# Identity and mask built by the vector engine, and new durations in the table that orders the instructions (linear attention and two gated MLPs, one core)

## The chip, the core and the metric

The kernel runs on one NeuronCore of a Trainium2 chip. A core has five engines that run side by side, each with its own instruction queue in order: TensorE (PE, matrix products, its weight loads are shown as PEld), VectorE (DVE), ScalarE (ACT), GpSimd (POOL) and SyncE (SP, which here issues all DMAs). They wait for each other through semaphores. The metric is the device time of one execution in microseconds (us).

## The reference

Three stages follow each other. Attention with a decaying state, per batch and head (4 batches, 8 heads, 768 steps, head dimension 48):

```
for t in range(S):
    state = alpha[:, :, t, :, None] * state + einsum('bhd,bhe->bhde', k[:, :, t], v[:, :, t])
    y[:, :, t] = einsum('bhd,bhde->bhe', q[:, :, t], state)
```

Then 3072 tokens of width 384 go through `x / rms * rms_g`, and `(silu(xn @ w_gate) * (xn @ w_val)) @ w_out` with an inner width of 1536, and then through `max(x @ w1, x @ w2, x @ w3) @ w_out` with an inner width of 768. All data is float32; the weights lie in memory as 64-bit numbers.

## The kernel before

**Attention** is done in 24 tiles of 128 time steps (6 for each of 4 batches, batches alternating). For a tile, the decays, keys and queries are loaded (`in_al`, `in_kk`, `in_qq`). For tiles 0 to 5 PE turns them (L570, transposes against `ident`); from tile 6 on DVE turns them (L576). DVE then runs a backward product scan (L598, writes `R`) and scales the keys (L604); this step is called `br`. The step `b` is a reciprocal, a forward scan (L611) and the scaling of the queries (L621). PE turns the keys back (L637) and forms the scores (L644); DVE masks them with `mask` (L657, `at`); PE multiplies with the values (L667, L676, L682), which gives the tile's output and the state's update (DVE L701 or L705). ACT sums the squares of the output, POOL makes the inverse root from it (L693, L696), DVE normalises (L710, `xn`), PE turns the tile (L716), and ACT and DVE split it into a high and a low half, `xh` (L723) and `xl` (L727).

**The first MLP** works on blocks of 384 tokens, which are three tiles. It goes through 96 slots; in a slot PE forms the gate product (nine matrix products, three splits over three parts of the width, L760 with `wg`), the value product (L760 with `wv`) and, later, the second product (L807). Between them ACT applies silu (L790), DVE multiplies (L793, tile `sg`), and ACT (L797) and DVE (L801, tile `hl`) split the result. The first two blocks alternate: slots 0 to 5 are block 0 with the first six of twelve column groups, slots 6 to 11 block 1 with the same six, slots 12 to 23 both with the other six. **The second MLP** has 48 slots of three products and a second product (L960).

**Weights** come in as chunks of 64-bit words (`raw`, L360). DVE rebuilds a float from each word (three instructions a chunk, L58 to L60, done for two chunks at once and called a join), ACT rounds it to the high half (L374), DVE makes the low half (L380), and ACT checks ranges (L389, L392).

**What sets the order.** Nothing in the kernel issues in the order of the loops. Every step is entered in a table with `plan.add(name, engine, cost, due, needs, run, ...)`; `Order.run` plays the table through with these costs: whenever an engine is free it takes the step with the lowest due time among those whose needs are met. The order in which steps start in this play is the order in which each engine's instructions are issued. On the chip each engine then follows its list strictly. Where PE would be free before the value product of slot 0, the play inserts a filler product (L767, a product of `ident` and `mask` whose result is not used) and reckons 0.11 us for it.

**The constants.** `ident` and `mask` (the upper triangle with the diagonal) are made on POOL by two library helpers: a memset each, and a select along a diagonal (masks.py:199 and masks.py:66). In POOL's list a row `ISA` stands ahead of the first select; it is the only one of its kind between the kernel's start and the last reduction.

Of the kernel before, what the change touches and what calls it, by code (L numbers as in the profile page):

```python
# [10 lines left out]

F32 = mybir.dt.float32
F32R = mybir.dt.float32r
# [5 lines left out]
ALU = mybir.AluOpType  # L19
# [4 lines left out]
B, H, S, D = 4, 8, 768, 48  # L24
DM, F1, F2 = 384, 1536, 768
P = 128
# [255 lines left out]
def gla_moe_moe(ctx: ExitStack, tc: tile.TileContext, q, k, v, alpha, wg, wv, wo, g, w1, w2, w3, wo2, out):  # L282
    nc = tc.nc
# [29 lines left out]
    plan = Order()  # L313
# [8 lines left out]
    class Weights:  # L322


        def __init__(self, tag, pool, bufs, chunks, where, due, needs):

            self.tag, self.pool, self.raws, self.tmps = tag, pool, {}, {}
            self.chunks, self.where = chunks, where
            n = len(chunks)
            first = tag == "w1"  # L330
            for i in range(n):
                at = due(i) - 10 - (HEAD[i // 2] if first and i < 8 else 1.5)
                before = needs(i) + self.prev("load", i, 1) + self.prev("check", i, bufs)
                if i >= bufs:
                    before.append((tag, "join", (i - bufs) // 2 * 2))
                plan.add((tag, "load", i), "SP", 1.1, at, before, partial(self.load, i, bufs), later=LAT)
            for i in range(0, n, 2):
                both = [j for j in (i, i + 1) if j < n]
                at = due(i) - (HEAD[i // 2] if first and i < 8 else 1 if first else 1.5)
                plan.add((tag, "join", i), "DVE", 1.3 * len(both), at,  # L340
                         [(tag, "load", j) for j in both] + self.prev("rest", i, 2) + self.prev("join", i, 2),
                         partial(self.join, both))
                plan.add((tag, "high", i), "ACT", 0.42 * len(both), at, [(tag, "join", i)] + self.needed(needs, both),
                         partial(self.high, both))
                plan.add((tag, "rest", i), "DVE", 0.47 * len(both), at + 0.2, [(tag, "high", i)],
                         partial(self.low, both))
                for j in both:
                    plan.add((tag, "check", j), "ACT", 1.14, at + 2, [(tag, "load", j)],
                             partial(self.check, j))

        def prev(self, kind, i, n):
# [72 lines left out]
    pa = ExitStack()  # L424
    ap1 = pa.enter_context(tc.tile_pool(name="ap1", bufs=1, side="right", reuse_waits="tile"))
    ap = pa.enter_context(tc.tile_pool(name="ap", bufs=2, side="right", reuse_waits="tile"))

    ident = ap1.tile([P, P], F32, name="ident")
    mask = ap1.tile([P, P], F32, name="mask")
    half = ap1.tile([P, 1], F32, name="half")  # L430
    gb = ap1.tile([P, DM], F32, name="gb")
    ins, halves = [], []
    for nm, fill in (("al", 1.0), ("kk", 0.0), ("qq", 0.0)):
        t = ap1.tile([P, 2 * H * 64], F32, name=f"in_{nm}")
# [10 lines left out]
    for t in (R, ends):  # L445
        nc.gpsimd.memset(t[:, :, P - 1:P], 1.0)
    St = [ap1.tile([W, NP, D], F32, name=f"S{b}") for b in range(B)]
    make_identity(nc, ident)
    make_upper_triangular(nc, mask, val=1.0, diag=True)
    nc.gpsimd.memset(half, -0.5)  # L450
    xh, xl = {}, {}
    order = list(range(8))
# [12 lines left out]
    def room(n):  # L465
        def count(_, started):
            return 3 if ("g", 0) in started else 6 if n >= TPB else 7
        return count
# [7 lines left out]
    class Tile_:  # L476


        def __init__(self, n):
            self.n, self.s, self.c0 = n, n % 2, n * NSTAT  # L480
            self.b, self.c = tiles[n]
            self.blk, self.j = divmod(n, TPB)
            c, last = self.c, self.c == NC - 1

            if n < TPB:
                at, step = -20 + 2 * n, 0.5
            elif n < 2 * TPB:
                at, step = -10 + 0.5 * (n - TPB), 1
            elif n < 3 * TPB:
                at, step = 12 + 3 * (n - 2 * TPB), 1  # L490
            else:
                at, step = 21 + 4 * (n - 3 * TPB), 0.7

            def t(kind, m=n):
                return ("t", kind, m) if m >= 0 else None

            def add(kind, engine, cost, i, needs, run, **kw):
                last_one = t(kind, n - 1)
                needs = needs + [last_one if last_one in plan.parts else None]
                plan.add(t(kind), engine, cost, at + step * i, needs, run, **kw)  # L500

            r = room(n)
            self.pe = n < NPE
            if n <= NPE:
                old = [t("pa", n - 2), t("pa", n - 1) if n == NPE else None]
            else:
                old = [t("bt", n - 1)]
            add("ld", "SP", 3.3, -2, old, self.load, later=LAT)
            add("lv", "SP", 1.1, -1, [t("pc", n - 2), t("ld")], self.load_v, later=LAT)
            if self.pe:  # L510
                plan.add(t("pa"), "PE", 1.31, at + 0.5, [t("ld"), t("pa", n - 1), t("pc", n - 2)], self.pe_a, banks=3,
                         until=[t("b")], room=r)
            free = [t("b", n - 1), t("pb", n - 2), t("pc", n - 2), t("sqb", n - 2)]
            if not self.pe:
                add("bt", "DVE", 1.85, 0.9, [t("ld")] + free, self.pre_bt)
            add("br", "DVE", 1.6, 1, [t("pa" if self.pe else "bt")] + free, self.pre_br)
            add("b", "DVE", 2.1 if c else 1.8, 1, [t("br")] + ([t("st", n - B)] if c else []) +
                ([t("st", n - 2)] if n < NT - B + 2 else []), self.pre_bq)
            add("sqb", "ACT", 1.48, 1.5, [t("b")], self.post_b)
            add("pb", "PE", 1.75 if last else 2.13, 1.5, [t("b"), t("pc", n - 1)], self.pe_b,  # L520
                banks=2 if last else 3, until=[t("c")] + ([] if last else [t("kn")]), room=r)
            if not last:
                add("kn", "ACT", 0.45, 2, [t("pb"), t("pc", n - 1)], self.copy_kn)
            add("c", "DVE", 1.25, 2, [t("pb"), t("pc", n - 1)], self.pre_c)
            add("pc", "PE", (1.4 if c else 0.9) + (0 if last else 0.5), 2.5,
                [t("c"), t("lv"), None if last else t("kn")], self.pe_c, banks=1 if last else 2,
                until=[t("d")] + ([] if last else [t("st")]), room=r)
            add("ss", "ACT", 0.42, 3, [t("pc")], self.norm)
            add("rr", "POOL", 0.6, 3, [t("ss")], self.root)
            if not last:  # L530
                add("st", "DVE", 0.54, 3, [t("pc")], self.pre_st)
            add("d", "DVE", 0.5, 3.1, [t("rr"), t("pc"), t("pd", n - 3), "gb"], self.pre_d)
            free = [("v", last_of[self.blk - 2])] if self.blk > 1 else []
            add("pd", "PE", 0.33, 3.5, [t("d")] + free, self.pe_d, banks=1, until=[t("el")], room=r)
            add("eh", "ACT", 0.42, 4, [t("pd")], self.split_h)
            add("el", "DVE", 0.47, 4, [t("eh")], self.split_l)
# [358 lines left out]
    n = len(chunks1)  # L895
# [10 lines left out]
    for blk in range(NBLK):  # L906
# [5 lines left out]
        at = NS + (blk - 1) * NF2 + 1 if blk else NS - 6  # L912
        final = max(pi for pi, p_ in enumerate(passes) if p_[0] == blk)
        if blk > 1:
            free = ("p", (blk - 1) * NF2 - 1, 2)
        else:
            free = ("v", last_of[NBLK - 2 + blk])
        plan.add(("yf", blk), "SP", 1.64, at, [("yst", final, i) for i in range(KT)] + [free] +
                 ([("yf", blk - 1)] if blk else []), fetch, later=2.2)
        for i in range(KT):  # L920
# [8 lines left out]
            n = blk * KT + i  # L929
# [120 lines left out]
```

## Time and profile before

| | us |
|---|---|
| median of 3 runs | 926.93 |
| lowest and highest of them | 926.07, 927.68 |
| the profiled execution's own time | 927.05 |
| its span (first to last instruction) | 925.2 |
| PE busy | 888.6 (96%) |
| DVE busy | 527.4 (57%) |
| ACT busy | 353.4 (38%) |
| POOL busy | 24.3 (3%) |

The span is 1.85 us shorter than the execution's time. The busy shares are means over stages with different limits: in the first 100 us DVE is busy almost without a gap, later PE is. In the chain of work that ended last, PE holds 84% and DVE 7%.

### The profile page before, as it was taken

To read this page: it belongs to the slowest core of one execution; us is meant where nothing else is said; L and a number is where in the kernel's file an instruction comes from. 1 tells how busy PE (TensorE), PEld (TensorE's weight loads), DVE (VectorE), ACT (ScalarE), POOL (GpSimd) and SP (SyncE) were. 2 spreads that over 40 slices of the span, in tenths; PEclk is the share of its full clock that TensorE was granted. 3 is DMA by queue.
4 is the path that set the end of the run, shared out by engine and by line. 5 is a ranking of instruction groups with operands and counts; after the bars stand their busy time and mean duration, and the time that the engine had idled before them with its cause. 6 is when DMAs were issued, how large, how long until landed. Compare 5 with 4: busy or idle time off the path is not lost.

```text
span 925.2 us, 16299 instructions
## 1 busy us (share of the span) xinstructions
PE 888.6 (96%) x6477; PEld 864.7 (93%) x6477; DVE 527.4 (57%) x1052; ACT 353.4 (38%) x898; POOL 24.3 (3%) x70
## 2 busy tenths in 40 slices
PE   4899699899999999999999999999999999999997
PEld 3789699799999999999999999999999999999997
DVE  3999978987666666666666258465333323323222
ACT  3568577432333333333223258553222212212121
POOL 1001000000000000000000000000000000000000
PEclk9999799999999999999999999999999999999999
DMA  8745454533223223222221025221100101101000
GB/s 170 130 125 172 129 187 120 146 108 82 56 57 82 57 56 83 56 57 82 57 56 53 1 86 182 92 99 39 52 26 27 52 1 52 39 13 52 1 26 28
DMA packets 106241, 69.14 MB, mean 75 GB/s; under 512 B 49200, under 2 KB 103856, under 8 KB 106160
## 3 DMA queue, kind: packets, MB, share of 16 engines
q1 hardware_dynamic: 106160, 68.05, 26.8%
q8 instruction: 52, 0.85, 0.4%
q14 instruction: 29, 0.24, 0.1%
HBM read 57.41 MB, written 10.62 MB: 74 GB/s over the span
## 4 chain that ended last, share of the span: by engine, by line
PE 84%; DVE 7%; DMA 2%; ACT 1%; issue 1%; POOL 0%; SPq 0%; DVEq 0%; POOLq 0%; ACTq 0%
PE bank L760 53%; PE bank L807 14%; PE bank L960 8%; PE bank L644 2%; PE bank L682 2%; PE bank L676 2%; DMA raw<-in_moe_w_dram 1%; DMA raw<-in_moe_w_val_dram 1%; PE bank L667 1%; DVE cv_t L59 1%; PE bank L716 1%; DVE aT L611 1%; DVE cv_t L60 1%; PE bank L637 1%; DVE sg L793 1%
## 5 line engine op out<-in xcount | busy, mean ns | idle before, releaser
L945 DVE TENSOR_TENSOR sg<-sg,bank 128x384 f32<-128x384 f32 x96 | 53.2, 554 | 171.6 <-PE bank L760 168.3
L793 DVE TENSOR_TENSOR sg<-sg,bank 128x384 f32<-128x384 f32 x96 | 52.8, 551 | 104.2 <-PE bank L760 103.5
L797 ACT ACTIVATE hh<-sg 128x384 fp32r<-128x384 f32 x96 | 50.2, 523 | 150.6 <-DVE sg L793 150.5
L760 PE MATMUL bank<-xh,wvh 128*128 128x384 f32 x288 | 98.7, 343 | 7.3 <-DVE sg L793 4.3
L760 PE MATMUL bank<-xh,wgh 128*128 128x384 f32 x288 | 100.8, 350 | 0.0
L760 PE MATMUL bank<-xh,wvl 128*128 128x384 f32 x288 | 97.7, 339 | 1.6 <-DVE wvl L380 1.6
L760 PE MATMUL bank<-xh,wgl 128*128 128x384 f32 x288 | 97.2, 337 | 1.5 <-DVE wgl L380 1.5
L807 PE MATMUL bank<-hh,woh 128*128 128x384 f32 x288 | 98.5, 342 | 0.0
L807 PE MATMUL bank<-hl,woh 128*128 128x384 f32 x288 | 96.7, 336 | 1.8 <-DVE hl L801 1.8
L760 PE MATMUL bank<-xl,wvh 128*128 128x384 f32 x288 | 97.4, 338 | 0.0
L760 PE MATMUL bank<-xl,wgh 128*128 128x384 f32 x288 | 97.1, 337 | 0.0
L807 PE MATMUL bank<-hh,wol 128*128 128x384 f32 x288 | 96.4, 335 | 0.0
L949 ACT ACTIVATE hh<-sg 128x384 fp32r<-128x384 f32 x48 | 25.2, 525 | 160.2 <-DVE sg L945 160.2
L801 DVE TENSOR_TENSOR hl<-sg,hh 128x384 fp32r<-128x384 f32 x96 | 53.3, 555 | 32.1 <-ACT hh L797 32.1
L790 ACT ACTIVATE sg<-bank 128x384 f32<-128x384 f32 x96 | 46.6, 486 | 47.2 <-PE bank L760 46.7
L760 PEld LDWEIGHTS bank<-xh,wvh 128*128 128x128 f32 x288 | 54.8, 190 | 9.8 <-DVE sg L793 6.4
L760 PEld LDWEIGHTS bank<-xh,wvl 128*128 128x128 f32 x288 | 54.9, 191 | 2.2 <-DVE wvl L380 2.2
L807 PEld LDWEIGHTS bank<-hl,woh 128*128 128x128 f32 x288 | 54.1, 188 | 2.7 <-DVE hl L801 2.7
L760 PEld LDWEIGHTS bank<-xh,wgl 128*128 128x128 f32 x288 | 54.6, 190 | 1.8 <-DVE wgl L380 1.8
L807 PEld LDWEIGHTS bank<-hh,woh 128*128 128x128 f32 x288 | 54.2, 188 | 2.0
L760 PEld LDWEIGHTS bank<-xh,wgh 128*128 128x128 f32 x288 | 54.8, 190 | 1.3
L760 PEld LDWEIGHTS bank<-xl,wvh 128*128 128x128 f32 x288 | 54.9, 191 | 0.0
(137 smaller groups left out, 2004.3 us busy)
## 6 DMA issues: line engine op xcount, KB each, us to landing
raw<-in_moe_w_out_dram SPq DMA_DIRECT2D x18, 384.0 KB, 3.9
raw<-in_moe_w_dram SPq DMA_DIRECT2D x18, 384.0 KB, 3.9
y_scr<-yo SPq DMA_DIRECT2D x30, 192.0 KB, 2.0
raw<-in_moe_w_gate_dram SPq DMA_DIRECT2D x12, 384.0 KB, 4.0
vt<-in_v_dram SPq DMA_DIRECT2D x24, 192.0 KB, 2.6
raw<-in_moe_w_val_dram SPq DMA_DIRECT2D x12, 384.0 KB, 3.8
xl<-y_scr SPq DMA_DIRECT2D x8, 576.0 KB, 4.3
out_dram<-yo SPq DMA_DIRECT2D x24, 192.0 KB, 1.9
```

The costliest lines, as they stand in the source:

```text
L644: nc.tensor.matmul(self.sc[i][:, pr, :], self.kT[lo:hi, pr, :], self.qT[lo:hi, pr, :], start=True, stop=True)
L676: nc.tensor.matmul(self.y[tk, 2 * pr:2 * pr + 2, :].rearrange("p a d -> p (a d)"), self.qT[:, pr, tk], Sds[self.s][:, pr, :], start=True, ...
L682: nc.tensor.matmul(self.y[tk, 2 * pr + i, :], at[i][:, pr, tk], vt[:, 2 * pr + i, :], start=not self.c, stop=True, skip_group_check=True,)
L760: nc.tensor.matmul(ps, w_[:, kt, col], m_[:, kt, :], start=i == 0, stop=i == 3 * KT - 1)
L790: nc.scalar.activation(hid[s], banks[3][:, :NB], AF.Silu)
L793: nc.vector.tensor_tensor(hid[s], hid[s], banks[4][:, :NB], ALU.mult)
L797: nc.scalar.activation(hi_[s], hid[s], AF.Copy)
L801: nc.vector.tensor_tensor(lo_[s], hid.pop(s), hi_[s].bitcast(F32), ALU.subtract)
L807: nc.tensor.matmul(banks[e][:, :NB], w_[:, f, es], m_, start=f == f0 and i == 0, stop=f == f1 - 1 and i == 2)
L945: nc.vector.tensor_tensor(hid2[z], hid2[z], banks[3 + j][:, :NB], ALU.max)
L949: nc.scalar.activation(hi2[z], hid2[z], AF.Copy)
L960: nc.tensor.matmul(banks[t][:, :DM], l_[:, tsl], r_[:, f, :], start=f == 0 and i == 0, stop=f == NF2 - 1 and i == 2)
```

## The change

`ident` and `mask` are built on DVE instead of POOL. A row of ones is scanned into a running count `column` (0, 1, 2, ... along the free dimension), a 32-wide transpose of it gives each partition its own number within a group of 32 (`place`), and for each group of 32 partitions one comparison writes the group's rows of `ident` (equal) and one those of `mask` (greater or equal). That is one memset, one scan, one transpose and eight comparisons on DVE; the two helpers' instructions leave POOL.

The second part changes costs in the table: eleven numbers, no need, due time or buffer.

```diff
-    make_identity(nc, ident)
-    make_upper_triangular(nc, mask, val=1.0, diag=True)
+    column = ap1.tile([P, P], F32, name="column")
+    place = ap1.tile([P, 32], F32, name="place")
+    nc.vector.memset(mask, 1.0)
+    nc.vector.tensor_tensor_scan(column, mask, mask, -1.0, ALU.mult, ALU.add)
+    nc.vector.transpose(place, column[:, 0:32])
+    for t, op in ((ident, ALU.is_equal), (mask, ALU.is_ge)):
+        for lo in range(0, P, 32):
+            nc.vector.tensor_scalar(
+                t[lo:lo + 32], column[lo:lo + 32], float(lo), place[lo:lo + 32, 0:1], ALU.subtract, op
+            )
...
-            add("br", "DVE", 1.6, 1, [t("pa" if self.pe else "bt")] + free, self.pre_br)
+            add("br", "DVE", 2.3, 1, [t("pa" if self.pe else "bt")] + free, self.pre_br)
...
-            add("sqb", "ACT", 1.48, 1.5, [t("b")], self.post_b)
+            add("sqb", "ACT", 1.95, 1.5, [t("b")], self.post_b)
```

The other costs: a chunk's high half 0.42 to 0.45, its check 1.14 to 1.42, `b` 2.1 to 2.7 (1.8 to 2.15 for a batch's first tile), `c` 1.25 to 1.2, `ss` 0.42 to 0.65, `rr` 0.6 to 0.85, `st` 0.54 to 0.75, `d` 0.5 to 0.54.

What this does to the lists, at three places. First POOL's list at the start (`half` is a constant of one column, `r` the inverse root of a tile). Before, and then after:

```order
L446 MEMSET ends 112x4
masks.py:197 MEMSET ident 128x128
masks.py:199 ISA
masks.py:199 AFFINE_SELECT ident<-ident 128x128
masks.py:65 MEMSET mask 128x128
masks.py:66 AFFINE_SELECT mask<-mask 128x128
L450 MEMSET half 128x1
L693 TENSOR_SCALAR r<-stats 128x1
```

```order
L446 MEMSET ends 112x4
L459 MEMSET half 128x1
L702 ISA
L702 TENSOR_SCALAR r<-stats 128x1
L705 TENSOR_TENSOR r<-r,half 128x1
```

The `ISA` row stands now ahead of the first inverse root. It waits for no semaphore; the instruction behind it waits for ACT.

Second, DVE's list ahead of the first gate product, which needs the third tile's `xl`. Before, with tile 4's steps `br` and `b` whole ahead of `xl`, and after (line numbers are 9 higher):

```order
L598 SCALAR_TENSOR_TENSOR R<-bank_74,ends 112x511
L603 TENSOR_SCALAR least<-R 112x4
L604 TENSOR_TENSOR kT<-bank_75,R 112x512
L608 RECIPROCAL starts<-least 112x4
L610 TENSOR_TENSOR all<-all,least 112x4
L611 SCALAR_TENSOR_TENSOR aT<-bank_74,starts 112x512
L617 TENSOR_TENSOR Sd_117<-S_125,all 48x4x48 x2
L621 TENSOR_TENSOR qT<-bank_78,aT 112x512
L727 TENSOR_TENSOR xl<-bank_76,xh 128x3x128
```

```order
L607 SCALAR_TENSOR_TENSOR R<-bank_74,ends 112x511
L612 TENSOR_SCALAR least<-R 112x4
L613 TENSOR_TENSOR kT<-bank_75,R 112x512
L736 TENSOR_TENSOR xl<-bank_79,xh 128x3x128
L617 RECIPROCAL starts<-least 112x4
L619 TENSOR_TENSOR all<-all,least 112x4
L620 SCALAR_TENSOR_TENSOR aT<-bank_74,starts 112x512
L626 TENSOR_TENSOR Sd_117<-S_125,all 48x4x48 x2
L630 TENSOR_TENSOR qT<-bank_78,aT 112x512
```

Tile 4's step `b` has moved behind that `xl`. On PE the fillers ahead of the first gate product are 191 instead of 141.

Third, DVE's list around the multiplication of slot 5 (the row with `sg`), which PE's value product of slot 6 waits for. Before and after:

```order
L380 TENSOR_TENSOR wvl<-cv_t,wvh 128x3x128
L380 TENSOR_TENSOR wol<-cv_t,woh 128x384
L58 TENSOR_SCALAR cv_t<-raw 128x384 x2
L59 SCALAR_TENSOR_TENSOR cv_t<-raw,cv_t 128x384 x2
L60 SCALAR_TENSOR_TENSOR cv_t<-raw,cv_t 128x384 x2
L608 RECIPROCAL starts<-least 112x4
L610 TENSOR_TENSOR all<-all,least 112x4
L611 SCALAR_TENSOR_TENSOR aT<-aT,starts 112x512
L617 TENSOR_TENSOR Sd_117<-S_127,all 48x4x48 x2
L621 TENSOR_TENSOR qT<-qT,aT 112x512
L793 TENSOR_TENSOR sg<-sg,bank_77 128x384
L380 TENSOR_TENSOR wgl<-cv_t,wgh 128x3x128
```

```order
L380 TENSOR_TENSOR wvl<-cv_t,wvh 128x3x128
L380 TENSOR_TENSOR wol<-cv_t,woh 128x384
L58 TENSOR_SCALAR cv_t<-raw 128x384 x2
L59 SCALAR_TENSOR_TENSOR cv_t<-raw,cv_t 128x384 x2
L60 SCALAR_TENSOR_TENSOR cv_t<-raw,cv_t 128x384 x2
L736 TENSOR_TENSOR xl<-bank_80,xh 128x3x128
L802 TENSOR_TENSOR sg<-sg,bank_77 128x384
L585 STREAM_TRANSPOSE aT<-in_al 128x4x4x32
L585 STREAM_TRANSPOSE kT<-in_kk 128x4x4x32
L585 STREAM_TRANSPOSE qT<-in_qq 128x4x4x32
L380 TENSOR_TENSOR wgl<-cv_t,wgh 128x3x128
L380 TENSOR_TENSOR wvl<-cv_t,wvh 128x3x128
```

All of tile 6 (three transposes, `br` and `b`) stood ahead of the multiplication of slot 5 before; now all of it stands behind.

On PE, what lies between the score products of tile 4 (L644) and the gate product of slot 3 was, before, the second and value products and then tile 4's value products and a turn (L667 to L716); after the change the gate product of slot 3 follows the scores of tile 4 at once.

## Rows read from the trace of the kernel before

**Rows 1.** The page: busy time, share of the span, instructions of PE
```profile
PE 888.6 (96%) x6477; PEld 864.7 (93%) x6477; DVE 527.4 (57%) x1052; ACT 353.4 (38%) x898; POOL 24.3 (3%) x70
```
**Rows 2.** PE's waits, 0 to 60 us: us in all, times, longest
```profile
PE bank L570 <- POOL ident masks.py:199: 13.7, 1, 13.7
```
**Rows 3.** Timeline of POOL: start, duration, instruction, idle before and its releaser
```profile
13.31 0.28 POOL masks.py:199 TENSOR_SCALAR_AFFINE_SELECT ident<-ident 128x128 f32<-128x128 f32 x1 [9.64 <-issue]
...
26.19 0.19 POOL L693 TENSOR_SCALAR r<-stats 128x1 f32<-128x1 f32 x1 [12.02 <-ACT junk L471]
```
**Rows 4.** Timeline of SP's DMA issues at the start
```profile
0.74 0.45 SPq L542 DMA_DIRECT2D in_al<-in_alpha_dram  x1
...
11.41 0.43 SPq L561 DMA_DIRECT2D vt<-in_v_dram  x1
14.78 0.37 SPq L542 DMA_DIRECT2D in_al<-in_alpha_dram  x1
```
**Rows 5.** DMA issues, 0 to 2.5 us: count, KB each, us to landing
```profile
in_al<-in_alpha_dram SPq DMA_DIRECT2D x1, 192.0 KB, 3.3
```
**Rows 6.** Timeline of DVE up to the first gate product
```profile
14.79 0.16 DVE L595 COPY all<-bank 112x4 f32<-112x4 f32 x1 [14.79 <-PE bank L570]
...
15.20 1.22 DVE L598 TENSOR_TENSOR_SCAN R<-bank,ends 112x511 f32<-112x511 f32 x1
...
19.27 0.62 DVE L58 TENSOR_SCALAR cv_t<-raw 128x384 int32<-128x384 int32 x2
...
20.74 1.02 DVE L60 SCALAR_TENSOR_TENSOR cv_t<-raw,cv_t 128x384 int32<-128x384 int32 x2
...
53.25 0.17 DVE L608 RECIPROCAL starts<-least 112x4 f32<-112x4 f32 x1
...
55.93 0.55 DVE L727 TENSOR_TENSOR xl<-bank,xh 128x384 fp32r<-128x384 f32 x1
```
**Rows 7.** Busy time of L767 alone: stretch, length, PE, PEld, clock, DMA, GB/s
```profile
0.00:56.70 56.70, 18.52 (x141) 14.41 (x141) 0.97 0.72 147
```
**Rows 8.** Busy time of all engines: PE, PEld, DVE, ACT, POOL, then clock
```profile
0.00:60.00 60.00, 42.25 (x492) 37.09 (x492) 42.89 (x92) 28.90 (x83) 6.74 (x27) 0.97 0.68 139
```
**Rows 9.** Timeline of PE: the first gate product
```profile
56.72 0.42 PE L760 MATMUL bank<-xh,wgh 128*128 128x384 f32 x1
```
**Rows 10.** PE's waits, 56 to 200 us
```profile
PE bank L760 <- DVE sg L793: 3.4, 2, 3.0
PE bank L760 <- ACT wvh L374: 2.8, 1, 2.8
PE bank L760 <- DVE wvl L380: 1.6, 1, 1.6
PE bank L760 <- DVE wgl L380: 1.5, 1, 1.5
PE bank L807 <- DVE hl L801: 1.5, 2, 1.3
```
**Rows 11.** The chain that ended last: start, duration, what
```profile
109.06 6.12 PE bank L760 x18
...
116.75 3.12 PE bank L760 x18
```
**Rows 12.** Busy time of all engines, columns as in rows 8
```profile
100.00:105.00 5.00, 3.54 (x11) 3.54 (x12) 3.49 (x10) 1.87 (x6) 0.00 (x0) 0.52 0.95 258
...
200.00:300.00 100.00, 100.00 (x838) 96.88 (x838) 68.39 (x132) 33.10 (x85) 2.95 (x8) 1.00 0.30 78
```
**Rows 13.** Timeline of DVE around the multiplication of slot 5
```profile
93.43 1.09 DVE L576 STREAM_TRANSPOSE aT<-in_al 128x512 f32<-128x512 f32 x1
...
105.77 0.17 DVE L608 RECIPROCAL starts<-least 112x4 f32<-112x4 f32 x1
...
108.46 0.55 DVE L793 TENSOR_TENSOR sg<-sg,bank 128x384 f32<-128x384 f32 x1
```
**Rows 14.** PE's waits, 200 us to the end
```profile
PE bank L807 <- DVE hl L801: 0.4, 1, 0.4
```

More of the change, by code (lines that the diff above doesn't have):

```diff
@@ L9 @@
 from concourse.bass import ds
-from concourse.masks import make_identity, make_upper_triangular
+from concourse.masks import make_identity
 F32 = mybir.dt.float32
@@ L342, in __init__ @@
                          partial(self.join, both))
-                plan.add((tag, "high", i), "ACT", 0.42 * len(both), at, [(tag, "join", i)] + self.needed(needs, both),
+                plan.add((tag, "high", i), "ACT", 0.45 * len(both), at, [(tag, "join", i)] + self.needed(needs, both),
                          partial(self.high, both))
@@ L347, in __init__ @@
                 for j in both:
-                    plan.add((tag, "check", j), "ACT", 1.14, at + 2, [(tag, "load", j)],
+                    plan.add((tag, "check", j), "ACT", 1.42, at + 2, [(tag, "load", j)],
                              partial(self.check, j))
@@ L515, in __init__ @@
                 add("bt", "DVE", 1.85, 0.9, [t("ld")] + free, self.pre_bt)
-            add("br", "DVE", 1.6, 1, [t("pa" if self.pe else "bt")] + free, self.pre_br)
-            add("b", "DVE", 2.1 if c else 1.8, 1, [t("br")] + ([t("st", n - B)] if c else []) +
+            add("br", "DVE", 2.3, 1, [t("pa" if self.pe else "bt")] + free, self.pre_br)
+            add("b", "DVE", 2.7 if c else 2.15, 1, [t("br")] + ([t("st", n - B)] if c else []) +
                 ([t("st", n - 2)] if n < NT - B + 2 else []), self.pre_bq)
-            add("sqb", "ACT", 1.48, 1.5, [t("b")], self.post_b)
+            add("sqb", "ACT", 1.95, 1.5, [t("b")], self.post_b)
             add("pb", "PE", 1.75 if last else 2.13, 1.5, [t("b"), t("pc", n - 1)], self.pe_b,
@@ L523, in __init__ @@
                 add("kn", "ACT", 0.45, 2, [t("pb"), t("pc", n - 1)], self.copy_kn)
-            add("c", "DVE", 1.25, 2, [t("pb"), t("pc", n - 1)], self.pre_c)
+            add("c", "DVE", 1.2, 2, [t("pb"), t("pc", n - 1)], self.pre_c)
             add("pc", "PE", (1.4 if c else 0.9) + (0 if last else 0.5), 2.5,
@@ L527, in __init__ @@
                 until=[t("d")] + ([] if last else [t("st")]), room=r)
-            add("ss", "ACT", 0.42, 3, [t("pc")], self.norm)
-            add("rr", "POOL", 0.6, 3, [t("ss")], self.root)
+            add("ss", "ACT", 0.65, 3, [t("pc")], self.norm)
+            add("rr", "POOL", 0.85, 3, [t("ss")], self.root)
             if not last:
-                add("st", "DVE", 0.54, 3, [t("pc")], self.pre_st)
-            add("d", "DVE", 0.5, 3.1, [t("rr"), t("pc"), t("pd", n - 3), "gb"], self.pre_d)
+                add("st", "DVE", 0.75, 3, [t("pc")], self.pre_st)
+            add("d", "DVE", 0.54, 3.1, [t("rr"), t("pc"), t("pd", n - 3), "gb"], self.pre_d)
             free = [("v", last_of[self.blk - 2])] if self.blk > 1 else []
```

## The prediction

> **What bounds the kernel now.** I read the page's busy times first. PE holds 96% of the span [rows 1], so what can be won is PE's idle time, its fillers, and stretches at a low clock; the useful products stay as they are. Then PE's waits. The longest by far is the first: 13.7 us until `ident` is there [rows 2]. POOL's timeline tells why: ahead of the select that writes `ident` POOL is idle for 9.64 us and waits for nothing that the profile shows [rows 3]; the only thing between its memset and the select is the `ISA` row of its list. The inputs come much earlier: the first tile's `in_al` is issued at 0.74 and lands 3.3 later, at 4.04 [rows 4, 5].
>
> From there DVE runs the first tiles. It starts at 14.79 [rows 6] and the first gate product, slot 0, at 56.72 [rows 9]; from 0 to 60 us DVE is busy for 42.89 of the 45.2 us that it has left then [rows 6, 8]. So the head is DVE's, with PE filled up by 141 fillers [rows 7]. After slot 0 PE waits 3.4 + 2.8 + 1.6 + 1.5 + 1.5 = 10.8 us up to 200 us, all of it for steps that DVE makes or feeds [rows 10], and pays for these waits a second time in clock: a piece of 18 products takes 6.12 us right after such a wait and 3.12 later [rows 11], 3.0 us more, which is the lower of the two clock levels (1.2 instead of 2.4 GHz); from 100 to 105 us the granted clock is 0.52 for 3.54 us of PE work [rows 12], some 1.7 us more. Together 15.5 us lost after slot 0. Behind 200 us PE is full, with DVE at 68% [rows 12] and one wait of 0.4 us of note [rows 14]; nothing is to be won there.
>
> **Part 1, the constants.** DVE's eleven instructions stand at the head of its list, where it is idle until 14.79. None is in the trace, so bounds from its own rows: a scan of 511 columns takes 1.22 and a transpose of 512 columns 1.09, a comparison-like operation on 384 columns 0.31 (two in 0.62) [rows 6, 13]. Taken whole, memset, scan, transpose and four comparisons for `ident` are at most 1.22 + 1.22 + 1.09 + 4 x 0.31 = 4.8 us; scaled by columns (128, 128, 32, 128) they are about 0.3 + 0.3 + 0.1 + 0.4 = 1.1. I take 2, near the scaled end, since the operands are a quarter as wide. With a start at about 0.7 `ident` is there near 3 (at most 5.5). PE then waits for the inputs, 4.04, and starts 9.6 us earlier than at 13.7 [rows 2]. The cover of the new work is thus the first load; if the upper bound holds it costs 1.5 us. `mask` follows within another us and is needed only after the first scores.
>
> What is late next? Two sums, of which the larger sets slot 0.
> DVE: it starts 14.79 - 13.7 = 1.1 after PE, at 5.2. Before, from 14.79 to the end of the third `xl` (55.93 and 0.5) it took 41.6 us [rows 6]. Tile 4's step `b`, 53.25 to 55.93, now stands behind that `xl`: 41.6 - 2.7 = 38.9, so 44.1, and a little more for the second weight chunk, whose landing now comes after DVE is ready for it.
> PE: from 13.7 to 56.72 it was busy for 42.25 less the 3.3 us past slot 0's start, 39.0, of which 18.52 were fillers: 20.5 us of work [rows 7 to 9]. There are 50 fillers more, at 18.52 / 141 = 0.13 or less each, 5 to 6.5 us: 20.5 + 18.5 + 6 = 45 from 4.04, so 49. Part of the old 39.0 ran at the low clock (the mean of 0.97 over 60 us is 1.8 us of it) and would shrink with more fillers: 47.2. I take 47.5 for slot 0, PE's own sum with its fillers as the bound: 9.2 us earlier. Both ends stay for the range: 45 and 49.
>
> **Part 2, the order.** The clearest row is the multiplication of slot 5, at 108.46, for which PE waited 3.0 us and after which it ran at half clock [rows 10, 11, 13]. Ahead of it in DVE's list stood all of tile 6: three transposes from 93.43 on (about 0.95 each, 2.8), and `br` and `b`, 4.5 us as for tile 0 from 14.79 to 19.27 [rows 6, 13]; the first row of `b` is at 105.77. These 7.3 us now stand behind it. Of the waits of [rows 10] the 3.0, 2.8 and 1.6 all lie in this stretch (95 to 109 us) and all come from this order: DVE did tile 6 while the weights for slot 5 waited. They go, with the clock that they cost.
>
> In their place others come, since DVE's total is the same. The one that I can work out is the gate product of slot 3. From the multiplication of slot 1 DVE has ahead of that slot's low halves one join (19.27 to 21.76, 2.5), tile 5's `br` and `b` (4.5, and 0.7 for the carried state), a multiplication, a low half and two low halves of weights (0.5 each): 9.7 us [rows 6]. PE has meanwhile what is left of slot 2's gate product (1.4), a second and a value product (1.56 each, half of 3.12 [rows 11]) and tile 4's scores (1.6): 6.1. It then waits 3.5 us where before it had tile 4's value products to do. Following the lists on in the same way I find four more waits of 0.6 to 1.7 us up to slot 17, 4.5 us in sum, an estimate. So 15.5 - 8.0 = 7.5 us won, if the clock holds through the 3.5 us; if it falls, 3.0 less. At least nothing is won, at most 15.5.
>
> **Sum.** Against the profiled execution's own 927.05 us (its span is 925.2; the median of the runs is 926.93, 0.1 less): 9.2 for the head and 7.5 for the order give 910.4; against the median 910.3. I forecast 910.3.
>
> **A rule weighed.** The `ISA` row now stands right ahead of the first inverse root and has no wait of its own. By the trace it began as soon as POOL's memsets were done and took 9.64 us [rows 3]; beginning at about 3.5 it is over at 13, and the first inverse root, at 26.19 before, is due at about 19 then: hidden. The Trainium skill (GPSIMD Engine Reference, 2.1 Instruction dispatch) says that the first call of a freshly loaded kernel pays about 6 us for loading its code. If that is paid at the call, it falls on the first inverse root's path, which is the fourth rival below. The trace before cannot tell the two apart, since there the call stood right behind the `ISA` row.
>
> **Rivals.**
> 1. The order wins nothing: as much new waiting as old. Then only the head is left, 927.05 - 9.2 = 917.9. For it: DVE's sum up to 100 us is unchanged, and a busy DVE makes one wait of another. Against: 7.3 us of work really leave the way of slot 5.
> 2. The new costs fit so well that no wait after slot 0 is left: 927.05 - 9.2 - 15.5 = 902.4. Against: slot 3's 3.5 us.
> 3. The start is the loads'. The third tile's loads, issued at 14.78, were held by PE's first transposes; now they follow the issue at 11.41 on SP [rows 4], 2.9 us earlier and no more. If everything hangs on them, 924.1. Against: that tile's transposes ran long after its loads had landed.
> 4. The POOL code is loaded at its first call. The first `xn` on DVE, which stands in order ahead of tile 2, comes 9.64 - 0.5 = 9.1 us late and takes the head's gain: 927.05 - 9.2 + 9.1 - 7.5 = 919.4, and 3.0 more for the clock of an idle PE, 922.4.
> 5. Slower: the order of the later stage is worse. Behind 200 us PE waits for next to nothing, and the new costs move `xl` ahead of a `hl` there (0.5 us a tile). If each of the 16 last attention tiles made PE wait for `hl` by as much as the longest such wait before, 1.3 us [rows 10], it would lose 20.8: 931.1. It decides from (16.7 + 1.9) / 16 = 1.2 us a tile on. Against: DVE's 32% of idle time there [rows 12] and a single wait of 0.4 [rows 14].
>
> **How the numbers follow.** Chances: the forecast (906 to 914) 0.47, rival 1 (to 921) 0.24, rival 2 (below 906) 0.14, rival 3 0.05, rival 4 0.05, rival 5 0.05. A measurement of this kernel tells 0.2%, 1.9 us, from no change. Faster by more: all of the forecast, of rivals 1, 2 and 4, and most of 3: 0.93; within 0.2%: 0.03; slower: 0.04. The range for 8 in 10 goes from 901.5 (slot 0 at 45 or so and few waits) to 922 (rival 1 with slot 0 at 49 and a lost clock). The likeliest case alone is 906 to 914.
>
> **What would show it.** In the profile after: no wait of PE for POOL, and PE's first transposes at 4 to 4.5 us; POOL's idle time of some 9.6 us ended by about 13, ahead of the first inverse root; the first gate product between 45 and 49; PE's waits from there to 200 us at 8 us in sum, with the longest at slot 3's gate product; the multiplication of slot 5 some 16 us earlier than 108.46. The forecast is wrong if the first inverse root shows an idle time ended by nothing, if slot 0 comes after 51, or if waits for `hl` appear behind 200 us.

## The result and the profile after

The changed kernel takes 905.64 us (median of 4 runs, 905.13 to 906.29) against 926.50 (4 runs) beside it: a ratio of 0.9774, 95% interval 0.9757 to 0.9791, so 2.1 to 2.4% faster. The profiled execution took 905.86 with a span of 903.7. The forecast was 910.3, with a range of 901.5 to 922 and 906 to 914 for the likeliest case; the result lies 0.4 below that last range, in the band that the prediction gave to its rival 2 (below 906, chance 0.14). In this document the head is the stretch up to slot 0's gate product.

The kernel after has nine lines more, so line numbers from 446 on are nine higher. First the page's busy times of after, as in [rows 1]:

```profile
PE 886.8 (98%) x6527; PEld 864.9 (96%) x6527; DVE 530.5 (59%) x1063; ACT 350.4 (39%) x898; POOL 22.5 (2%) x66
```

PE's idle time is 16.9 us (903.7 - 886.8) where it was 36.6. PE's waits of after, first for 0 to 60 us, which answer to [rows 2]:

```profile
PE bank L579 <- DMA in_al<-in_alpha_dram: 4.3, 1, 4.3
PE bank L676 <- ACT kn L659: 1.2, 1, 1.2
PE bank L676 <- ACT junk L389: 0.9, 1, 0.9
PE bank L653 <- DVE aT L620: 0.3, 1, 0.3
```

The 13.7 us for POOL are gone. PE starts at 4.27, when the first load lands, 9.4 us earlier. DVE's timeline at the start shows the new work, which ends `ident` at 3.8, and POOL's the first inverse root, to be held against [rows 3]:

```profile
1.03 0.42 DVE L452 TENSOR_TENSOR_SCAN column<-mask 128x128 f32<-128x128 f32 x1
1.49 0.21 DVE L453 STREAM_TRANSPOSE place<-column 128x32 f32<-128x32 f32 x1
1.74 2.04 DVE L456 TENSOR_SCALAR ident<-column,place 32x128 f32<-32x128 f32 x4
3.81 1.16 DVE L456 TENSOR_SCALAR mask<-column,place 32x128 f32<-32x128 f32 x4
```
```profile
3.71 0.13 POOL L459 MEMSET half<- 128x1 f32 x1
19.14 0.19 POOL L702 TENSOR_SCALAR r<-stats 128x1 f32<-128x1 f32 x1 [15.30 <-ACT junk L480]
```

POOL's idle time ahead of the inverse root is ended by ACT and not by "issue": whatever took 9.64 us before is over by 19.14, if it came at all, and nobody waits for it. No row of either trace shows the `ISA` row itself.

Next comes slot 0's gate product, against [rows 9], with the chain ahead of it. ACT's check of a weight chunk waits for its load. Tile 3's sums of squares stand behind it in ACT's list. DVE's `starts` of tile 4 overwrites what they read. PE's scores of tile 3 want a bank that DVE's scan of tile 4 has to leave (start, duration, instruction, idle before):

```profile
43.18 0.56 ACT L389 ACTIVATE junk<-raw 128x384 bf16<-128x384 f32 x1 [4.59 <-DMA raw<-in_moe_w_val_dram]
44.48 0.47 ACT L732 ACTIVATE xh<-bank 128x384 fp32r<-128x384 f32 x1
44.85 0.62 ACT L480 ACTIVATE junk<-kT 112x512 bf16<-112x512 f32 x1
```
```profile
44.98 0.56 DVE L736 TENSOR_TENSOR xl<-bank,xh 128x384 fp32r<-128x384 f32 x1
46.67 0.18 DVE L617 RECIPROCAL starts<-least 112x4 f32<-112x4 f32 x1 [1.14 <-ACT junk L480]
46.89 1.22 DVE L620 TENSOR_TENSOR_SCAN aT<-bank,starts 112x512 f32<-112x512 f32 x1
```
```profile
48.17 1.16 PE L653 MATMUL bank<-qT,kT 48*128 48x128 f32 x14 [0.35 <-DVE aT L620]
49.25 0.44 PE L769 MATMUL bank<-xh,wgh 128*128 128x384 f32 x1
```

Slot 0 is 7.5 us earlier than at 56.72. From its start to the end the span took 925.2 - 56.72 = 868.5 before and takes 903.7 - 49.25 = 854.4 now, 14.0 less; 7.5 + 14.0 is the 21.5 by which the span fell. PE's waits of after from 45 to 200 us, against [rows 10], where the five rows came to 10.8:

```profile
PE bank L769 <- DVE xl L736: 1.2, 1, 1.2
PE bank L816 <- DVE hl L810: 1.1, 2, 0.9
PE bank L646 <- DVE aT L620: 0.8, 1, 0.8
PE bank L653 <- DVE aT L620: 0.3, 1, 0.3
PE bank L653 <- DVE qT L630: 0.3, 1, 0.3
```

They are 3.7 together. The row of L653 for `aT` is the 0.35 at 48.17, ahead of slot 0, so 3.4 are left behind it. The query of [rows 10] has two more rows, of 0.4 and 0.3 us, so 11.5 went down to 3.4. The longest wait now stands inside slot 6's gate product:

```profile
93.01 0.44 PE L769 MATMUL bank<-xl,wgh 128*128 128x384 f32 x1 [1.16 <-DVE xl L736]
```

The multiplication of slot 5 on DVE, at 108.46 in [rows 13], now stands ahead of tile 6's transposes, 15.6 us earlier; 7.5 of these are slot 0's, and 8.1 come behind it:

```profile
92.41 0.55 DVE L736 TENSOR_TENSOR xl<-bank,xh 128x384 fp32r<-128x384 f32 x1
92.87 0.54 DVE L802 TENSOR_TENSOR sg<-sg,bank 128x384 f32<-128x384 f32 x1
93.33 1.08 DVE L585 STREAM_TRANSPOSE aT<-in_al 128x512 f32<-128x512 f32 x1
```

The clock: before, 0.52 from 100 to 105 us [rows 12]; after, the one stretch behind slot 0 at a low clock is this (busy times with columns as in [rows 8], PE's third from the left, the clock third from the right):

```profile
65.00:70.00 5.00, 4.59 (x26) 3.89 (x27) 5.00 (x12) 2.97 (x9) 0.00 (x0) 0.71 0.59 178
70.00:75.00 5.00, 5.00 (x81) 4.70 (x80) 4.38 (x10) 4.87 (x16) 0.13 (x1) 0.95 0.51 161
```

4.59 x 0.29 + 5.00 x 0.05 makes 1.6 us lost, at slot 3.

Where the 14.0 us behind slot 0 arise can be read from the gate products, which come in the same order in both kernels. From slot 0's to slot 6's it took 47.1 us before and takes 42.3 now, 4.8 less. At slot 12's the gain has grown to 9.5, at slot 18's to 12.3, and at slot 24's, at 214.59 before and 194.60 now, to 12.5. The last 1.5 us come later.

### The profile page after: what moved, and what is told of

Its sections match the earlier page's. It is cut to its first block, busy times and chain, and to the rows that moved or that the text cites. A ratio compares the mean times of both kernels' runs of the same rounds, so it can differ in the third digit from the quotient of the medians.

```text
span 903.7 us, 16408 instructions
## 1 busy us (share of the span) xinstructions
PE 886.8 (98%) x6527; PEld 864.9 (96%) x6527; DVE 530.5 (59%) x1063; ACT 350.4 (39%) x898; POOL 22.5 (2%) x66
## 4 chain that ended last, share of the span: by engine, by line
PE 89%; DVE 4%; DMA 3%; SPq 2%; ACT 1%; issue 1%; DVEq 0%; ACTq 0%
PE bank L769 56%; PE bank L816 15%; PE bank L969 8%; PE bank L653 2%; PE bank L691 2%; PE bank L685 2%; DMA raw<-in_moe_w_val_dram 1%; PE bank L676 1%; DVE cv_t L59 1%; DVE cv_t L60 1%; SPq L551 1%; PE bank L776 1%; PE bank L725 1%; SPq L562 1%; PE bank L646 1%
## 5 line engine op out<-in xcount | busy, mean ns | idle before, releaser
L769 PEld LDWEIGHTS bank<-xl,wgh 128*128 128x128 f32 x288 | 54.5, 189 | 1.5 <-DVE xl L736 1.5
L816 PEld LDWEIGHTS bank<-hh,wol 128*128 128x128 f32 x288 | 54.2, 188 | 0.0
```

What stands on the lines that cost most here:

```text
L769: nc.tensor.matmul(ps, w_[:, kt, col], m_[:, kt, :], start=i == 0, stop=i == 3 * KT - 1)
L816: nc.tensor.matmul(banks[e][:, :NB], w_[:, f, es], m_, start=f == f0 and i == 0, stop=f == f1 - 1 and i == 2)
```

## The experiments

**Theory.** This is what the runs were to test. The two parts are independent: the constants move the start, and the order decides what follows slot 0; within the order it is the place of tile 6's work on DVE. The head is shorter by less than the start because ACT's checks wait for loads. **Rivals.** The order's gain needs the early start; truer durations are worth something in any order they give; PE's fillers set slot 0.

**One part alone.** The first run has only the constants, the second only the durations:

```diff
-    make_identity(nc, ident)
-    make_upper_triangular(nc, mask, val=1.0, diag=True)
+    nc.vector.memset(mask, 1.0)
+    nc.vector.tensor_tensor_scan(column, mask, mask, -1.0, ALU.mult, ALU.add)
...
```


> Constants made by DVE, all the old durations in the ordering model, so the order of before (141 fillers). If the two parts add up: PE starts at about 4.3 instead of 13.7, slot 0's gate product comes at 47.5 to 49.3 (56.72 before), and from there on the 868.5 us of before follow unchanged: 917.5 to 919.5. If the loads held the head (rival 3 of the prediction): 924. If the order of before makes DVE late again at once, so that the earlier start is lost in its waits up to 110 us: 922 to 926.

```diff
-            add("ss", "ACT", 0.42, 3, [t("pc")], self.norm)
-            add("rr", "POOL", 0.6, 3, [t("ss")], self.root)
+            add("ss", "ACT", 0.65, 3, [t("pc")], self.norm)
+            add("rr", "POOL", 0.85, 3, [t("ss")], self.root)
...
```


> New durations in the ordering model, constants still made by POOL. If the two parts add up: PE starts at 13.7 again, slot 0's gate product comes at 57 to 58.7 (49.25 of after plus up to 9.4; 50 fillers more than before), and from there on 854.4 us as in after: 913.5 to 915.5. If the new order is only good with the early start, because its loads and its DVE list fit only then: 918 to 925. If the prediction's term for the order was right (7.5) and the rest of the gain came from the head: 919.4.

Constants alone: 918.35 us, ratio 0.9916 (0.9886 to 0.9947), span 916.3. Durations alone: 913.16, ratio 0.9868 (0.9837 to 0.9898), span 910.5. The first gate product of either, constants first:

```profile
48.25 0.42 PE L769 MATMUL bank<-xh,wgh 128*128 128x384 f32 x1
```
```profile
56.20 0.44 PE L760 MATMUL bank<-xh,wgh 128*128 128x384 f32 x1
```

From there to the end it is 916.3 - 48.25 = 868.1 with the old order and 910.5 - 56.20 = 854.3 with the new. So the stretch behind slot 0 depends on the order alone (868.5 and 854.4 in the two kernels): the order's gain does not need the early start. Ahead of slot 0 the constants bring 8.5 in the old order and 7.0 in the new (56.20 to 49.25), so there the parts add only to within 1.5 us.

**Tile 6 put back ahead of slot 5's multiplication**, by a change of the finished list of after:

```diff
+        out.remove(('t', 'bt', 6))
+        out.insert(out.index(('t', 'el', 5)) + 1, ('t', 'bt', 6))
+        out.remove(('t', 'br', 6))
+        out.insert(out.index(('t', 'bt', 6)) + 1, ('t', 'br', 6))
+        out.remove(('t', 'b', 6))
+        out.insert(out.index(('t', 'br', 6)) + 1, ('t', 'b', 6))
```


> The changed kernel with one piece of the order undone: DVE does tile 6's three transposes, br and b ahead of the multiplication of slot 5, as in before; all else stays. If this piece is what cost before: the multiplication comes some 7.3 us later than 92.87, at about 100; PE has only slot 6's gate product (1.56) meanwhile, waits about 5.5 us and runs at the lower clock behind it (1.5 to 3 us); of that DVE gives back up to 4 later (the hl waits of 4.0 us in sum in after). So 909 to 914. If the place of tile 6 is worth nothing, since DVE has to do the work somewhere: 905 to 907.

914.37 us, ratio 0.9875 (0.9845 to 0.9905), span 912.4, beyond the range of its first case by 0.4 and far from the second. DVE, PE and the busy times (columns as above) of this run:

```profile
92.81 1.11 DVE L591 STREAM_TRANSPOSE aT<-in_al 128x512 f32<-128x512 f32 x1
...
100.56 0.55 DVE L808 TENSOR_TENSOR sg<-sg,bank 128x384 f32<-128x384 f32 x1
```
```profile
101.16 0.69 PE L775 MATMUL bank<-xh,wvh 128*128 128x384 f32 x1 [6.52 <-DVE sg L808]
```
```profile
100.00:125.00 25.00, 23.84 (x122) 23.84 (x123) 16.38 (x37) 17.35 (x48) 0.00 (x0) 0.86 0.40 118
```

Moving three steps of one tile brings a wait of 6.52 and 3.3 us at the low clock (23.84 x 0.14). The stretch behind slot 0 is 912.4 - 49.62 = 862.8 long: this one piece costs 8.4 us in the new list. It costs them between slot 6's gate product and slot 12's (37.4 us, against 28.4 in after and 33.1 before); up to slot 6's this run is as fast as after (41.8 us). So the 4.8 us won up to slot 6 have another cause in the order, which no run took apart, and that 8.4 of before's 14.0 hang on tile 6 is not shown. The reverse, tile 6 moved back in the list of before, was not run.

**ACT's checks moved back**, three and then four of them:

```diff
+        out.remove(('w1', 'check', 2))
+        out.insert(out.index(('t', 'kn', 0)) + 1, ('w1', 'check', 2))
+        out.remove(('w1', 'check', 4))
+        out.insert(out.index(('t', 'ss', 1)) + 1, ('w1', 'check', 4))
+        out.remove(('w1', 'check', 7))
+        out.insert(out.index(('t', 'sqb', 3)) + 1, ('w1', 'check', 7))
```


> The changed kernel with three of ACT's checks of weight chunks moved a few places back in ACT's list: number 2 behind kn of tile 0, number 4 behind the sum of squares of tile 1's output, number 7 (which waited 4.59 us for its load) behind tile 3's squares. If these checks made slot 0 late (PE waits of 1.2, 0.9 and 0.35 us ahead of it, DVE's 1.14 for starts): slot 0's gate product at 46.9 to 48.4 instead of 49.25, and the whole 903.2 to 904.8. If PE's own sum with its 191 fillers holds slot 0: 49.2 and 905.6, the same within 0.2%.

```diff
+        out.remove(('w1', 'check', 3))
+        out.insert(out.index(('t', 'kn', 1)) + 1, ('w1', 'check', 3))
```


> As the run with three checks moved, with number 3 moved as well, behind kn of tile 1. There number 3 waited 3.90 us for its load and held xh of tile 0, DVE's xl (2.20) and the bank that PE's product of tile 1 needs (3.38). If that is why the three moves won nothing: these waits go, slot 0 comes at 47 to 48.6 instead of 49.25 (51.14 with three moves), and the whole is 903.2 to 905.0. If another load takes their place (the DMA engines are 79% busy up to 60 us): 905 to 907.

Three moves: 907.12 us, span 905.0, slot 0 at 51.14 and nothing won. The check that had not been moved shows why. It waited 3.90 us for its load (1.52 in after; why this load came later is not shown) and held `xh` of tile 0, for which DVE waits. Behind DVE's scan PE waits for a bank: the profile names no releaser, but PE starts 0.1 after that scan ends, at 28.58, and by the list it writes the bank that the scan reads:

```profile
25.49 0.56 DVE L742 TENSOR_TENSOR xl<-bank,xh 128x384 fp32r<-128x384 f32 x1 [2.20 <-ACT xh L738]
...
27.36 1.22 DVE L626 TENSOR_TENSOR_SCAN aT<-bank,starts 112x512 f32<-112x512 f32 x1
```
```profile
28.69 0.74 PE L682 MATMUL bank<-vt,kn 128*48 128x48 f32 x16 [3.38 <-issue]
```

With the fourth moved the 2.20 is gone and slot 0 comes at 47.40, in a span of 901.6:

```profile
47.40 0.44 PE L777 MATMUL bank<-xh,wgh 128*128 128x384 f32 x1
```

Behind it follow 854.2 us. In the profiled executions the checks so account for the 1.9 us by which the head gained less (7.5) than the start (9.4). The runs had a median of 904.42 (902.9 to 906.5), ratio 0.9771 (0.9744 to 0.9799): the profile shows the 1.9 us at slot 0, but the times alone can't tell this kernel from after.

**Fillers.** First every second one left out of the finished list, then the same together with the four moved checks:

```diff
+        fills = [i for i, name in enumerate(out) if name is None]
+        for i in reversed(fills[1::2]):
+            del out[i]
```


> The changed kernel with every second of PE's 191 fillers left out, the order of all other work as it is. If PE's own sum with its fillers sets slot 0, as the prediction had it: 95 fillers of 0.11 less, some 10 us, so slot 0 comes when DVE's third xl is there, at 45 to 46.5 instead of 49.25, and the whole 902 to 904. If ACT's check number 7 sets it (it waits for its load until 43.18, xh, tile 3's squares, starts and aT follow): 48.5 to 49.3, and the whole 905 to 908, since the clock of an emptier PE may fall ahead of slot 0.

> The four moved checks and every second filler left out, together. Alone the checks gave slot 0 at 47.40 and a span of 901.6, the fillers 49.01 and 902.4. If DVE now sets slot 0 (third xl at 44.37, then starts, aT, tile 4's scores): 46.3 to 47.4, and from there 853.4 to 854.2, so a span of 900 to 901.6 and a time of 902 to 904. If the thinner head lets the clock fall ahead of slot 0: 905 to 907.

Half the fillers: 904.38 us, span 902.4, slot 0 at 49.01. PE waits more ahead of it instead (2.8, 2.3, 2.0 and 1.4 us) and the end of the head doesn't move, so the fillers are not what holds slot 0. Both together: 904.98 us, span 903.2, the same in time as the checks alone (904.42), with this at slot 0 in PE's timeline:

```profile
46.94 1.38 PE L664 MATMUL bank<-qT,kT 48*128 48x128 f32 x14 [1.38 <-DVE aT L631]
48.25 0.69 PE L780 MATMUL bank<-xh,wgh 128*128 128x384 f32 x1
48.74 0.52 PE L780 MATMUL bank<-xl,wgh 128*128 128x384 f32 x1
```

The products run in 0.52 instead of 0.34 us: slot 0 starts at the lower clock (0.89 over 45 to 60 us; 1.00 with the checks moved and all fillers). That the missing fillers alone did this is not shown, for with half of them and the checks left in place the clock held over the same 15 us, with as little work on PE and the same wait of 1.4 us ahead of the scores:

```profile
45.00:60.00 15.00, 13.63 (x133) 12.77 (x132) 14.35 (x34) 11.00 (x32) 0.74 (x2) 1.00 0.29 83
```

**`ident` made twice.**

```diff
-    for t, op in ((ident, ALU.is_equal), (mask, ALU.is_ge)):
+    for t, op in ((ident, ALU.is_equal), (ident, ALU.is_equal), (mask, ALU.is_ge)):
```


> The changed kernel with the four comparisons that write ident made twice (2.04 us more on DVE ahead of PE's start; the values are the same). In after ident was ready at 3.8 and the first load at 4.27. If the load covers only what is ready by then: PE starts at 5.8 to 6.0, slot 0 comes 1 to 1.7 later than 49.25, and the whole is 906.5 to 907.6. If ACT's checks and their loads set slot 0 whatever the start: slot 0 within 0.5 of 49.25, and 905.0 to 906.2.

906.38 us, span 903.8, and PE's first transposes:

```profile
5.58 1.07 PE L579 MATMUL bank<-ident,in_al 128*112 128x128 f32 x4 [5.58 <-DVE ident L456]
```

PE starts 1.3 later than at 4.27 and slot 0 comes at 50.09, 0.84 later, and the median is 0.7 higher, with runs that overlap: `ident` costs nothing only up to the landing of the first load. The profiled span hardly moved. In this execution the clock held at slot 3 (1.00 from 65 to 70 us against 0.71), which fits, but is no effect of the edit that could be shown.

**Other numbers in the ordering model**: a longer landing time; ACT's and POOL's five durations (`high`, `check`, `sqb`, `ss`, `rr`) as before and DVE's new; DVE's durations a little higher.

```diff
-    LAT = 2.2
+    LAT = 3.0
```


> The changed kernel with the ordering model's time from a load's issue to its landing at 3.0 instead of 2.2 us (the traces show 4.0 to 5.5 in the head, against 1.1 + 2.2 in the model); 119 fillers. If loads that land later than the model thinks make the head late: ACT's checks stand later in its list, the waits for loads of 1.5, 2.3 and 4.6 us shrink, slot 0 comes at 46 to 48, and the whole is 902 to 905. If the gain of the order hangs on the place of few pieces, which any change of a number moves: 906 to 915, with waits of PE between slots 1 and 6 over the 3.7 us of after.

```diff
-            add("sqb", "ACT", 1.95, 1.5, [t("b")], self.post_b)
+            add("sqb", "ACT", 1.48, 1.5, [t("b")], self.post_b)
...
```


> The changed kernel with only DVE's new durations in the model (br, b, c, st, d), those of ACT and POOL as before. In DVE's list tile 6 then stands ahead of the multiplication of slot 2, neither as in before (ahead of slot 5's) nor as in after (behind it); 128 fillers. If DVE's durations carry the order's gain: 904 to 908. If it is only the two sets together that put tile 6 in a good place: 910 to 918, with a long wait of PE at slots 2 to 4.

```diff
-            add("br", "DVE", 2.3, 1, [t("pa" if self.pe else "bt")] + free, self.pre_br)
+            add("br", "DVE", 2.4, 1, [t("pa" if self.pe else "bt")] + free, self.pre_br)
...
```


> The changed kernel with DVE's durations in the model 4 to 7% higher (br 2.4, b 2.8 and 2.25, c 1.25, st 0.8), nearly as true to the trace as the new ones. In DVE's list tile 6 then stands ahead of the multiplication of slot 3 instead of slot 6. If truer durations bring the gain in themselves: 904 to 908. If the gain is that of one lucky order among neighbours: 909 to 918, with waits of PE of 6 to 12 us in sum from slot 0 to 200 us (3.7 in after).

The longer landing time gives 924.73 us in 10 runs (ratio 0.9981, 0.9967 to 0.9994), slower than both of its cases; DVE's durations alone 914.85 (0.9883, 0.9859 to 0.9906), so they don't carry the gain; the higher ones 918.78 (0.9923, 0.9898 to 0.9948), just beyond its second case. The head is not the cause (slot 0 at 50.48, 45.74 and 47.71). The stretch behind it is, and its length sorts all the runs but the last one below. Each row is one execution; spans of one kernel went from 922.0 to 926.5 in the runs of before, from 903.0 to 904.2 in those of after, and from 900.8 to 904.4 with four checks moved, so differences of 1 or 2 us in the last column decide nothing:

| kernel | slot 0 at | span | slot 0 to end |
|---|---|---|---|
| before | 56.72 | 925.2 | 868.5 |
| constants alone | 48.25 | 916.3 | 868.1 |
| after | 49.25 | 903.7 | 854.4 |
| durations alone | 56.20 | 910.5 | 854.3 |
| four checks moved | 47.40 | 901.6 | 854.2 |
| half the fillers | 49.01 | 902.4 | 853.4 |
| three checks moved | 51.14 | 905.0 | 853.9 |
| four checks and half the fillers | 48.25 | 903.2 | 854.9 |
| `ident` twice | 50.09 | 903.8 | 853.7 |
| tile 6 put back | 49.62 | 912.4 | 862.8 |
| DVE's durations alone | 45.74 | 912.7 | 867.0 |
| durations 4 to 7% higher | 47.71 | 916.7 | 869.0 |
| loads at 3.0 | 50.48 | 921.7 | 871.2 |

In all kernels with 853 to 855 us DVE's list has tile 6's transposes behind the multiplication of slot 5, as after has. In the others they stand ahead of it: ahead of slot 5's before, with the constants alone and with tile 6 put back, ahead of slot 3's with the loads at 3.0 and with the higher durations, ahead of slot 2's with DVE's durations alone. This agrees with the theory and does not prove it, since the last three lists differ in more than tile 6.

The orders with other numbers have new waits up to 200 us. PE's three longest lines with the loads at 3.0, and with the durations 4 to 7% higher:

```profile
PE bank L769 <- ACT wvh L374: 2.7, 1, 2.7
PE bank L769 <- DVE wvl L380: 2.1, 1, 2.1
PE bank L676 <- ACT kn L659: 1.8, 2, 1.6
```
```profile
PE bank L816 <- DVE hl L810: 3.3, 2, 2.1
PE bank L769 <- DVE sg L802: 2.9, 1, 2.9
PE bank L646 <- DVE aT L620: 2.6, 1, 2.6
```

**The gate ahead of the scores** didn't test what it was to test:

> Four checks moved, every second filler left out, and slot 0's gate product ahead of tile 4's transposes and scores in PE's list, so that it needs only the third xl. If PE's time ahead of slot 0 is then waiting for DVE alone: gate at 44.9 to 45.5, the scores right behind the slot's products, and a span of 898.5 to 900.5 (900 to 902.5 timed). If it only swaps 1.6 us of scores with 1.6 us of products, and tile 4's values come late instead: a span of 900.5 to 902.5.

904.15 us, span 902.0. The move names tile 4, but the scores ahead of slot 0 are tile 3's (two expectations carry the same slip); tile 4's come behind slot 2. So slot 0's gate product went back behind slot 2's value product, and slot 0's multiplication takes another sum than its own: this kernel computes something else, and its time is no result for the theory. Whether the gate can usefully stand ahead of tile 3's scores stays open.

## Why the prediction was nearly right

The direction and both mechanisms held. The two terms were both mis-sized, in opposite directions: 9.2 for the head measured 7.5, and 7.5 for the order measured 14.0. That the sum missed by 4.8 us of span and not by 6.5 is luck. Of the prediction's signs, PE's start, the missing wait for POOL and the multiplication of slot 5 came as said. Slot 0 came 0.25 us behind its last bound of 49, and PE's waits behind it, 3.4 us where 8 were said, have their longest at slot 6 and not at slot 3.

**The start** held: 4.27 against 4.04, no wait for POOL. `ident` took 3 us of DVE (ready at 3.8) where 2 were taken, between the bounds. In after it was ready 0.5 before the load landed; in the run with the constants alone, whose first four comparisons took 2.47 instead of 2.04, PE's first wait ends with `ident`, also at 4.3.

**Slot 0.** 47.5 was PE's own sum with its fillers. DVE's third `xl` ended at 45.54, near what was worked out (44.1 and a little). From 4.27 to slot 0 PE was busy for 42.48 of 44.98 us, no more than the sum had (43.5 from 4.04 to 47.5). The term that it had at nothing is PE's waits, 2.5 us: 1.2, 0.9 and the 0.35. The sum missed that ACT stands in between: the check at 43.18 had waited 4.59 us for a load. The prediction said that the second weight chunk would land after DVE is ready for it, and priced it at "a little more"; it did not follow the checks, which ACT does in order, ahead of `xh` and the squares. With four checks moved slot 0 comes at 47.40, the predicted value, with one wait of 1.2 left. The halved fillers show that in after PE's sum was not what set it.

**The order.** What would go (15.5) was nearly right: the rows for `sg`, `wvh`, `wvl` and `wgl` in [rows 10], 9.3 us, are gone, and with them 5.0 us of low clock (worked out below). What would come was not: 8.0 us of new waits were forecast, and all waits behind slot 0 up to 200 us are 3.4, with 1.6 of low clock. At slot 3 the forecast was 3.5. DVE's side held (9.7 reckoned; 9.2 from 57.67 to 66.88), but PE had more to do. It was still at tile 5's transposes at 57.67 (to 58.51, 0.8), which were not counted; tile 4's turn and scores took 2.1 (64.29 to 66.70, less a wait of 0.31) where 1.6 were counted; and the first two products of a gate need no low half of the weights (0.5). So it waited 0.84 and 0.31 instead:

```profile
64.29 0.60 PE L646 MATMUL bank<-ident,kT 112*128 112x112 f32 x4 [0.84 <-DVE aT L620]
65.62 1.16 PE L653 MATMUL bank<-qT,kT 48*128 48x128 f32 x14 [0.31 <-DVE qT L630]
66.70 0.45 PE L769 MATMUL bank<-xh,wgh 128*128 128x384 f32 x1
```

The "four more waits, 4.5 us, an estimate" came to 2.3 (the `xl` and `hl` rows). Behind 200 us, where the prediction saw nothing to win, the query of [rows 14] lists two waits for `sg` beside the 0.4, 0.9 in sum; of these 1.3 us 0.2 are left. By the busy times behind slot 0, PE's idle time fell from 18.9 to 10.1 us and its busy time from 849.6 to 844.3: 8.8 of waits and 5.3 of faster work. The stretches with a low clock explain 3.4 of the 5.3 (busy time by what the clock lacked: 0.4 + 1.7 + 0.4 + 2.5 = 5.0 in the four 5 us from 95 to 115 before, 1.6 after); the remaining 1.9 are not placed.

**The rivals.** Rival 1, that the order wins nothing, is refuted by the run with the durations alone. Rival 2 (902.4) is nearer than the forecast in time, by 3.2 us against 4.7, and in its mechanism, with 3.4 us of waits left instead of none. Rival 3 is refuted by the constants alone (918.35 against 924). Rival 4 is refuted by the inverse root's row: had the 9.64 us fallen on the call, the row at 19.14 would be some 9 us late with no releaser. The Trainium skill (GPSIMD Engine Reference, 2.1 Instruction dispatch) says that the first call to a freshly loaded kernel pays for a load of code, about 6 us. In this trace no such time stands in front of the call; whether a load ran earlier, while POOL waited for ACT, no row shows. Rival 5 did not come: behind 200 us the `hl` wait is 0.2, where it was 0.4 in [rows 14].

## What to carry to other kernels

Follow every engine's list through a shortened head, checks and copies included: an in-order engine that waits for a DMA ahead of a step that others need passes its wait on. A table of durations is a way of picking an order, not a gain in itself: three other sets of numbers, one of them within 7% of these, gave back 12 us or more of the 14. So time the order that comes out, and keep the order. When a wait is forecast from two lists, start both at the same instant, with what each still has in hand.

## What was not expected of the hardware

DVE's comparisons were slow beside POOL's memsets. DVE's timeline in the run with `ident` made twice, the first of eight equal comparisons and two later ones:

```profile
1.74 1.44 DVE L456 TENSOR_SCALAR ident<-column,place 32x128 f32<-32x128 f32 x1
...
3.65 0.60 DVE L456 TENSOR_SCALAR ident<-column,place 32x128 f32<-32x128 f32 x2
```

The first began at 1.74 and took 1.44, while POOL's memsets of `ends`, `starts` and `Sd` ran from 1.75 to about 3.5; from 3.65 on, with POOL nearly done, they took about 0.3 each. In after the first four took 424 to 619 ns, and POOL's `Sd` memsets 0.93 for the two instead of 0.78 before. The Trainium skill (SBUF — State Buffer, Who interferes with whom) names `tensor_scalar` among the DVE operations that can enter a mode which takes the port pair shared with GpSimd, and says that whoever issues first holds the pair for the whole instruction while the other is blocked. The longer rows on both engines fit this; no run here shows whether these comparisons ran in that mode.

And the clock: after waits of 0.84 and 0.31 us it fell to half at slot 3 in after (products of 0.52 us from 67.97 on), and with the same two waits it held in the run with `ident` twice:

```profile
65.00:70.00 5.00, 4.38 (x31) 3.62 (x32) 4.96 (x13) 2.28 (x8) 0.00 (x0) 1.00 0.78 226
```

Two other executions of after had a mean clock of 0.999, as this run has, against 0.996 in the profiled one. So the fall need not belong to the kernel; what decides there is not shown.
